# Which engine waits for the last output stores: five waits on ScalarE in place of seventeen on SyncE

## The chip, the cores and the metric

The kernel runs on one core of one Trainium2 chip. A core has five engines with an instruction stream each: TensorE (PE, matrix products), VectorE (DVE), ScalarE (ACT), GpSimd (POOL) and SyncE (SP, which here only issues transfers and waits). They meet only through semaphores. Transfers run on DMA engines; SyncE and ScalarE each issue them into a queue of their own. The metric is the device time of one execution in microseconds, the median of several runs. Before the change it is 99.43 us.

## The reference

The inputs are x of 2048 x 640, wqkv of 640 x 1920 and wo of 640 x 640, all bf16. What is computed is a block of linear attention with 32 heads of 20 columns:

```python
qkv = (x @ wqkv).reshape(B, S, 3, H, Dh).transpose(2, 0, 3, 1, 4)
q, k, v = qkv[0], qkv[1], qkv[2]
phi = lambda t: where(t > 0, t + 1, exp(t)) + 1e-6
pq, pk = phi(q), phi(k)
kv  = einsum("bhsd,bhse->bhde", pk, v)
z   = einsum("bhsd->bhd", pk)
num = einsum("bhqd,bhde->bhqe", pq, kv)
den = einsum("bhqd,bhd->bhq", pq, z)[..., None] + 1e-6
out = (num / den).transpose(0, 2, 1, 3).reshape(B, S, D) @ wo
```

The output is 2048 x 640 in bf16, 2.62 MB.

## The kernel before

The 2048 rows are cut into 16 tiles of 128 rows (`st` = 0 to 15). The stages are: loading x, also transposed, and the weights; the keys and phi(k); the product of x with phi(k), summed over all rows; the queries and phi(q) with the denominators; a small matrix that joins kv and wo; and at the end the output tiles, phi(q) divided by the denominator times that small matrix.

Every instruction is recorded in a plan, class `Plan`, before any is emitted. `add` takes the engine, the tiles that are read and written, and whether it is a transfer. It works out which earlier instructions have to be over, and puts a wait only for those that the engine does not know to be over already. What an engine knows lies in `P.known[engine]`: for each semaphore the value that it has waited for, directly, or because an instruction that it waited for had itself waited for it. Each transfer has a semaphore of its own, which stands at 16 when all of it has landed. `emit` then writes out each engine's list in the order in which it was recorded: SyncE, GpSimd, ScalarE, VectorE, TensorE.

The output stage is what matters here. `out_tile` handles tiles 0 to 14: two products into two PSUM banks (`out_mm`, line 576), two copies into the staging buffer `osb[st % 4]` (`out_evac`, line 599 on ScalarE, line 602 on VectorE), and one store of 160 KB from SyncE's queue (`out_dma`, line 587). `out_last` handles tile 15 in four column ranges and two stores: columns 0 to 480 (120 KB) from SyncE's queue, and columns 480 to 640 (40 KB) from ScalarE's queue. Those are 17 stores, and `out_dma` notes the key of each in the list `out_keys`.

There are four staging buffers. So a copy for tile `st` has to wait until the store of tile `st - 4` has landed, and ScalarE, which copies a part of every tile, thereby comes to know that the stores of tiles 0 to 11 have landed. It does not come to know it of tiles 12, 13 and 14, nor of the two stores of tile 15.

After all lists are emitted, the last loop of the function (lines 730 to 732) adds a wait for each of the 17 stores to SyncE's program. The compiler puts two of these waits into one instruction where it can; in the profile line 732 has 9 instructions. ScalarE's program ends with the issue of the 40 KB store.

Of the kernel before, what the change touches and what calls it, by code (L numbers as in the profile page):

```python
# [84 lines left out]
def bass_standalone__linear_attn_block__prompt_kernel(nc, x, wqkv, wo, out):  # L85
# [15 lines left out]
    with contextlib.ExitStack() as ctx:  # L101
# [38 lines left out]
        P = Plan(nc, es)  # L140
# [588 lines left out]
            P.emit(name, eng)  # L729
        for key in out_keys:  # L730
            op = P.writers[key]
            nc.sync.wait_ge(P.sem_obj[op.sem], op.val)


# [26 lines left out]
```

## Time and profile before

| what | value |
|---|---|
| time, median of 3 runs | 99.43 us (99.40 to 99.69) |
| profiled execution, its own time | 99.56 us |
| profiled execution, span from first to last instruction of the kernel | 98.3 us |
| granted TensorE clock | 1.000 |
| TensorE busy | 95.1 us, 97% of the span |
| VectorE busy | 63.7 us, 65% |
| ScalarE busy | 48.8 us, 50% |

The profiled execution took 1.26 us more than its span: the span holds the kernel's own instructions, the time also holds something of what the runtime does ahead of them and behind them. The profile was taken by the hardware on one execution. The names PEq, ACTq, SPq and so on stand for an engine's sequencer, which carries out waits and issues transfers; such instructions are not counted as busy time. EVENT_SEMAPHORE is a wait as an instruction of its own, DMA_DIRECT2D is the issue of a transfer.

### The profile page before, as it was taken

What the parts mean: (1) busy time and instruction counts of PE and PEld (TensorE: products, weight loads), DVE (VectorE), ACT (ScalarE), POOL (GpSimd) and SP (SyncE); (2) the same over time, 40 slices, a digit from 0 to 9 for tenths busy, and PEclk for the clock granted to TensorE, in tenths of its full rate; (3) what the DMA queues carried; (4) which work ended last, traced back from release to release, by engine and by line L of the source; (5) the groups of instructions that cost most, each with busy time, mean ns of one, the idle gap of its engine ahead of it and who ended that gap; (6) DMA issues with size and microseconds to landing.
All of it is one profiled execution on the core that took longest, in us unless ns stands there. A gap on an engine that the chain in (4) does not pass through costs nothing.

```text
span 98.3 us, 1814 instructions
## 1 busy us (share of the span) xinstructions
PE 95.1 (97%) x694; PEld 61.2 (62%) x699; DVE 63.7 (65%) x124; ACT 48.8 (50%) x93; POOL 4.7 (5%) x19
## 2 busy tenths in 40 slices
PE   6999999999999999999999999999999999999991
PEld 2467777777755444445687867655557677777771
DVE  5314998888899439997839836758999206272222
ACT  5116455544526120005806456796988765453532
POOL 6500000000000000000000520000000000000000
DMA  2999999999998294000340023313200335532334
GB/s 48 320 269 194 238 157 111 350 366 360 316 169 108 21 239 80 0 0 0 63 77 7 0 63 93 94 32 86 79 0 0 133 74 168 205 117 87 130 133 137
DMA packets 26369, 12.60 MB, mean 128 GB/s; under 512 B 18553, under 2 KB 26361, under 8 KB 26361
## 3 DMA queue, kind: packets, MB, share of 16 engines
q1 hardware_dynamic: 25640, 11.87, 50.2%
q10 hardware_dynamic: 720, 0.61, 1.9%
q8 instruction: 5, 0.08, 0.3%
q14 instruction: 4, 0.02, 0.1%
HBM read 5.90 MB, written 2.62 MB: 87 GB/s over the span
## 4 chain that ended last, share of the span: by engine, by line
PE 95%; ACT 2%; issue 0%
PE ps L293 23%; PE ps L576 22%; PE ps L354 22%; PE ps L317 21%; PE ps L283 3%; ACT w2g L483 2%; PE ps L445 1%; PE ps L544 1%; PE ps L200 1%; PE ps L472 1%; ACT osb L599 0%
## 5 line engine op out<-in xcount | busy, mean ns | idle before, releaser
L317 PE MATMUL ps<-pk,xn 128*128 128x480 bf16 (+1 forms) x160 | 23.2, 299 | 0.0
L293 PE MATMUL ps<-wk,xT 128*128 128x320 bf16 x160 | 22.8, 303 | 0.0
L354 PE MATMUL ps<-xT,wqn 128*128 128x512 bf16 x95 | 22.0, 379 | 0.4 <-issue 0.2
L576 PE MATMUL ps<-w2p,pq 128*128 128x320 bf16 (+2 forms) x170 | 22.1, 291 | 0.0
L293 PEld LDWEIGHTS ps<-wk,xT 128*128 128x128 bf16 x160 | 15.6, 98 | 6.8 <-DMA wk<-in_wqkv_dram 0.9
L576 PEld LDWEIGHTS ps<-w2p,pq 128*128 128x128 bf16 x170 | 15.9, 98 | 6.2 <-issue 0.2
L317 PEld LDWEIGHTS ps<-pk,xn 128*128 128x128 bf16 x160 | 13.6, 98 | 9.4 <-issue 0.3
L362 ACT ACTIVATE eq<-ps 128x512 bf16<-128x512 f32 x20 | 11.9, 597 | 13.8 <-PE ps L354 13.6
L354 PEld LDWEIGHTS ps<-xT,wqn 128*128 128x128 bf16 x100 | 11.5, 118 | 9.1 <-issue 0.3
L306 ACT ACTIVATE ek<-ps 128x640 bf16<-128x640 f32 x16 | 11.2, 704 | 10.7 <-PE ps L293 10.1
L599 ACT CAST osb<-ps 128x320 bf16<-128x320 f32 (+2 forms) x27 | 11.0, 413 | 9.7 <-PE ps L576 9.0
L311 DVE SCALAR_TENSOR_TENSOR pk<-ps,ek 128x640 bf16<-128x640 f32 x16 | 13.2, 825 | 0.5
L569 DVE TENSOR_TENSOR pq<-pq,rd 128x512 bf16<-128x512 bf16 x20 | 7.3, 418 | 4.2 <-DMA rd<-rdc 4.2
L375 DVE TENSOR_SCALAR eq<-eq 128x512 bf16<-128x512 bf16 x20 | 5.8, 288 | 5.9 <-ACT eq L362 5.8
L602 DVE CAST osb<-ps 128x320 bf16<-128x320 f32 (+1 forms) x7 | 3.2, 456 | 8.7 <-PE ps L576 8.7
L308 DVE TENSOR_SCALAR ek<-ek 128x640 bf16<-128x640 bf16 x16 | 5.2, 325 | 5.3 <-ACT ek L306 5.1
L366 ACT ACTIVATE rq<-ps 128x512 bf16<-128x512 f32 x13 | 7.7, 592 | 0.0
L339 ACT CAST pt<-ps 128x480 bf16<-128x480 f32 x4 | 2.2, 562 | 8.2 <-PE ps L317 8.1
L379 DVE TENSOR_TENSOR pq<-eq,rq 128x512 bf16<-128x512 bf16 x13 | 5.5, 426 | 1.1 <-ACT rq L366 0.7
L388 DVE TENSOR_TENSOR za<-pk 128x1280 f32<-128x1280 bf16 x4 | 5.8, 1482 | 0.0
L382 DVE SCALAR_TENSOR_TENSOR pq<-ps,eq 128x512 bf16<-128x512 f32 x7 | 4.8, 692 | 0.2
L388 DVE TENSOR_TENSOR za<-za 128x1280 f32<-128x1280 f32 x3 | 4.4, 1486 | 0.0
(37 smaller groups left out, 36.7 us busy)
## 6 DMA issues: line engine op xcount, KB each, us to landing
out_dram<-osb SPq DMA_DIRECT2D x15, 160.0 KB, 1.8
xn<-in_x_dram SPq DMA_DIRECT2D x2, 640.0 KB, 8.9
xn<-in_x_dram SPq DMA_DIRECT2D x1, 960.0 KB, 7.0
wqn<-in_wqkv_dram SPq DMA_DIRECT2D x1, 800.0 KB, 5.6
wv<-in_wqkv_dram SPq DMA_DIRECT2D x5, 150.0 KB, 5.1
wog<-in_wo_dram SPq DMA_DIRECT2D x2, 375.0 KB, 5.3
w2p<-w2g SPq DMA_DIRECT2D x10, 75.0 KB
rd<-rdc SPq DMA_DIRECT2D x8, 64.0 KB, 2.1
```

The source lines that it names most:

```text
L293: r = e.matmul(bank(b + h, HALF), xT[:, c * S + 128 * st:c * S + 128 * st + 128], wk[:, c * D + HALF * h:c * D + HALF * (h + 1)], start=(c ...
L306: P.add("act", lambda e: e.activation(fold(t[:, :]), two_banks(b), ACTF.Exp), reads=banks + ["table"], writes=[("ek", st % 3)])
L311: P.add("dve", lambda e: e.scalar_tensor_tensor(fold(pk[:, st * D:(st + 1) * D]), two_banks(b), 0.0, fold(t[:, :]), ALU.max, ALU.add), rea ...
L317: return e.matmul(bank(d // PB[h], PW[h], off=PW[h] * (d % PB[h])), xn[:, st * D + 128 * d:st * D + 128 * d + 128], pk[:, st * D + PO[h]:s ...
L354: r = e.matmul(bank(b), wqn[:, d * D:(d + 1) * D].rearrange("p (q c) -> p c q", c=NC_)[:, c, :], xT[:, d * S + BK * sbk:d * S + BK * (sbk ...
L362: P.add("act", lambda e: e.activation(t[:, :], bank(b), ACTF.Exp), reads=[("bank", b), "table"], writes=[("eq", i)])
L366: P.add("act", lambda e: e.activation(r[:, :], bank(b), ACTF.Relu), reads=[("bank", b), "table"], writes=[("rq", i)])
L375: P.add("dve", lambda e: e.tensor_scalar(t[:, :], t[:, :], 1.0, 1e-6, ALU.min, ALU.add), reads=[("eq", i)], writes=[("eq", i)])
L388: P.add("dve", lambda e: e.tensor_tensor(d_ap, a, b, ALU.add), reads=ra + rb, writes=[dst])
L569: P.add("dve", lambda e: e.tensor_tensor(v, v, rd[i][:, BK * h:BK * (h + 1)], ALU.mult), reads=[("rd", i, 2 * h), ("rd", i, 2 * h + 1), (" ...
L576: r = e.matmul(bank(b, hi - lo), pq[:, c * S + 128 * st:c * S + 128 * st + 128], w2p[:, c * D + lo:c * D + hi], start=(c == 0), stop=(c == ...
L599: P.add("act", lambda e: e.copy(osb[j][:, lo:hi], bank(b, hi - lo)), reads=[("bank", b)], writes=keys)
```

## The change

The loop at the end of the function no longer waits on SyncE. For each of the 17 stores it asks whether ScalarE's knowledge already covers the store's landing; if so, no wait is written, and if not, ScalarE waits. What is left is five waits at the end of ScalarE's program, behind the issue of the 40 KB store. SyncE's program ends with the issue of the 120 KB store.

```diff
         for key in out_keys:
             op = P.writers[key]
-            nc.sync.wait_ge(P.sem_obj[op.sem], op.val)
+            if P.known["act"].get(op.sem, 0) >= op.val:
+                continue
+            nc.scalar.wait_ge(P.sem_obj[op.sem], op.val)
```

## The prediction

> **What bounds the kernel now.** I read the page first, for the span and the chain that ended last.
>
> ```profile
> span 98.3 us, 1814 instructions
> ...
> PE   6999999999999999999999999999999999999991
> ...
> PE 95%; ACT 2%; issue 0%
> ```
>
> TensorE fills every slice but the first and the last, and the chain that ended last is 95% TensorE. The change touches no TensorE instruction and nothing that one waits for. So only the last slice, some 2 us in which TensorE is done, can move. Next I read the instructions in order of time from 96.3 us on.
>
> ```profile
> 96.12 0.20 PE L576 MATMUL ps<-w2p,pq 128*128 128x80 bf16 x1
> 96.18 0.24 DVE L602 CAST osb<-ps 128x80 bf16<-128x80 f32 x1
> 96.36 0.23 ACT L599 CAST osb<-ps 128x80 bf16<-128x80 f32 x1
> 96.36 0.33 SPq L587 DMA_DIRECT2D out_dram<-osb  x1
> 96.67 0.35 ACTq L587 DMA_DIRECT2D out_dram<-osb  x1
> ```
>
> The last issue is ScalarE's, over at 96.67 + 0.35 = 97.02. Behind it only waits stand: line 732's own instructions, SyncE's waits in that stretch, and the issues with their times to landing.
>
> ```profile
> L732 SPq EVENT_SEMAPHORE  x9: 17/28/28, 96.8 to 98.3; - x9
> ```
>
> ```profile
> SPq L732 <- DMA out_dram<-osb: 0.5, 1, 0.5
> ```
>
> ```profile
> out_dram<-osb SPq DMA_DIRECT2D x1, 120.0 KB, 1.7
> out_dram<-osb ACTq DMA_DIRECT2D x1, 40.0 KB, 1.6
> ```
>
> The columns of the first are shortest/median/longest in ns and first and last start. The nine waits begin at 96.8 and the last at 98.3, where the span ends. The 40 KB store, issued at 96.67, lands 1.6 us later: 98.26 in the trace's landings (the 120 KB store at 98.09). Two steps of 16 and 28 ns follow, SyncE's last wait starting at 98.276 and over at 98.304. The landing of ScalarE's store, not the number of waits, ends the program.
>
> **Behind the span.** The profiled execution took 99.56 us, so 1.26 us lie around the span. Besides the views, the trace keeps a time for each semaphore update. Semaphore 2, which no line of the kernel uses, goes up nine times ahead of the kernel, nine times around its end and nine times after it (ns from the span's start, as the trace records them):
>
> ```
> ahead    -370  -336  -298  -254  -231  -118   -80   -46     1
> end     96498 97295 97333 97377 98436 98479 98517 98551 98599
> after   99387 99421 99460 99504 99527 99626 99664 99698 99745
> ```
>
> I read each line as a barrier in which the five engines sign in one after another and four of them again on the way back. In the line "end" the second step comes 271 ns after ScalarE's last issue (97024), and the fifth 132 ns after SyncE's last wait (98304), about 1.1 us behind the fourth. So the second signer is ScalarE and the fifth, the turning point, is SyncE; the first (96498, just behind the last matmul's update at 96336) is TensorE. Which of VectorE and GpSimd is third doesn't matter. From 98569 to 99163 a block of semaphore updates follows that the kernel does not make, the resets of about 50 semaphores by each engine; the last 50 end at 99163, long behind the others (98970), and belong to the first signer by their numbers (semaphores up to 53). So what follows starts from step nine.
>
> **The change part by part.**
>
> SyncE loses 9 wait instructions. Seven were over by 97.62, below 98.26; their 17 to 28 ns each are covered by the flight of the last stores. The eighth (98.104) is covered by the landing at 98.26. Removed: 0 on the path, except the last, which is replaced. Nothing is queued behind SyncE's waits in the kernel, so its earlier end releases no transfer. Its own sign-in stays behind the fourth.
>
> ScalarE gains five waits, 3 instructions if two are again put into one. Behind them on ScalarE stands no kernel instruction: its last copy and its last issue are ahead. So no copy, issue or buffer comes later. The waits for tiles 12 to 14 are for landings up to 97.27 (the third of them), covered by 98.26. The wait for the last store then ends as SyncE's did: 16 + at most 28 ns behind the landing, 98.304. Shown for single waits of the plan, the two engines' prices agree (17 ns on both):
>
> ```profile
> L81 ACTq EVENT_SEMAPHORE  x35: 17/17/17, 2.7 to 96.6; - x35
> L81 SPq EVENT_SEMAPHORE  x10: 17/17/17, 56.0 to 96.3; - x10
> ```
>
> So the span stays at 98.3, plus or minus 0.03.
>
> What moves is the last arrival at the barrier. Now SyncE comes last and is the fifth: after 132 ns to its step, four steps back, 98599 - 98436 = 163 ns. Together 295 ns. Afterwards ScalarE comes last and is the second: x ns to its step, then seven steps. The trace has no barrier that only ScalarE held up; the nearest rows are the two unhindered passes, where second to ninth took 1 + 336 = 337 and 99745 - 99421 = 324 ns, mean 330. (The step after the turn takes 113 and 99 ns there, since that engine has just signed; 43 where it had long been waiting, as at "end".) The difference is 330 + x - 295 = 35 + x ns.
>
> The x is not shown behind a wait. From below: one instruction, the shown gap of 40 ns behind an issue of ScalarE's and 17 ns, gives 57, so +0.09 us. From above: the 271 ns that ScalarE took in this trace, behind its issue, gives +0.31. SyncE's 132 behind a wait is the like case on the other engine and gives +0.17; ScalarE is quicker through the runtime's instructions elsewhere (from its step to its first reset 99 ns, SyncE 133), which would make x 99 and the sum +0.13. I take x = 115, between these two, because they are the rows behind a wait or a step; the 271 I put down to a store just issued, whose first packet started only at 97.55. That gives +0.15 us: 99.56 + 0.15 = 99.71 for the profiled execution, which stood 0.13 above the median of the runs; on the median 99.43 + 0.15 = **99.58**.
>
> Everything behind the ninth step keeps its length, since TensorE's resets are the longest and start from there; the covers that SyncE and ScalarE have for their own resets are 0.2 us and more.
>
> The Trainium skill speaks against this change as well: "Runtime: NRT & Kernel Launch", section "The ~15µs preamble/postamble breakdown", has the barrier as a serpentine over the five engines at 44 ns a hop, eight hops, about 355 ns. The trace's passes agree in the whole (371 and 358 ns) but not step by step (23 to 113 ns). By equal hops the move from fifth to second costs three hops, 132 ns, and the time would be 99.56; the page doesn't say which engine is where.
>
> **The rivals.**
>
> A: ScalarE's 271 ns are the runtime's work on ScalarE, whatever stands ahead of it. For it: it is the only row of ScalarE's arrival. Against it: ScalarE's other turnarounds are shorter than SyncE's. The mechanism is in the second step of the barrier, its price 271 + 35 = 306 ns, time 99.74, slower by 0.31%. It decides from x = 263 on, where the sum reaches 0.298 us.
>
> B: the time ends with the kernel's last instruction, or the barrier is not on its path. For it: I can't place the two ends of the 1.26 us. Against it: 99.56 is longer than from the span's start to the ninth step at "end" (98.60), and nothing in the trace lies in the 1.2 us just ahead of the first instruction but that barrier and four transfers of 40 bytes. Then only the wait's 28 ns are in play: 99.43, within 0.03.
>
> C: SyncE's waits slow the last landing. For it: one 8 KB fetch of instructions starts at 98.173, between SyncE's last two waits, and the last two increments of the 40 KB store's semaphore come 26 and 40 ns after the one ahead, where the others stand 8 to 20 ns apart. If SyncE's shorter program moves that fetch behind the landing, some 26 + 40 - 2 x 10 = 46 ns come back: 99.53. With the lower bound of x (57, +0.09) as well it is 99.47. Against a real gain: that is still no time below 99.43, and no row shows a larger saving.
>
> D: the waits push ScalarE's closing instructions over an edge of its instruction memory, and a fetch comes between. The 8 KB fetches took 0.31 to 0.51 us during the kernel (47.9, 49.6 and 98.2 us). That gives 99.9 to 100.1. Against it: three instructions are few, and a page is fetched ahead.
>
> **How the numbers follow.** About 0.3%, 0.30 us, is what a measurement of this kernel can tell from no change. The main case has 0.57 of the chance, A 0.22, B 0.13, C 0.04, D 0.04. The main case reaches from 99.52 (x = 57) to 99.66 (x midway to A), with the scatter of a median of 3 (the runs shown lie 99.40 to 99.69) from 99.46 to 99.74, so about 0.05 of its chance falls beyond 99.73. A lies on that edge: some 0.15 of its 0.22 fall beyond, the rest on this side. With D and a little scatter, slower has 0.27. Faster has no mechanism among these; scatter below B, and what I have not seen, get 0.06. Same: 0.67. The range runs from 99.40, which holds B with little scatter, to 99.79, which holds A; D and the tails are left out, about 1.5 in 10.
>
> **What the profile after would show.** No SyncE instruction behind its issue at 96.4 and three ScalarE waits, the last starting at 98.28: the edit. The span at 98.3: the landing sets it. Semaphore 2: the fifth step right behind the fourth, the second one 115 ns behind ScalarE's last wait, and second to ninth in 324 to 340 ns. If the second comes 271 ns behind, A holds. If all this holds and the time doesn't move, B does. A fetch between ScalarE's last wait and the second step is D. The prediction is wrong if the last store lands at another time, or if the ninth step moves by 0.3 us or more.

## The result, and the profile after

The changed kernel takes 100.12 us, the kernel before 99.69 us (medians of 22 runs each; the 99.43 of the first three runs was on the low side). The ratio is 1.0047, with a 95% interval of 1.0026 to 1.0067: some 0.3 to 0.7 us slower. When it was run again beside the experiments the ratio was 1.0030 [1.0006, 1.0054]. The forecast was +0.15 us, counted as no difference, with 0.27 for slower. Single slow runs, over 1.5% longer than the fastest of the same kernel, are left out of the ratios and of the means below.

Within the span nothing of weight moved. From the page of the changed kernel, the span, the engines' busy time and TensorE's slices:

```profile
span 98.3 us, 1813 instructions
...
PE 95.1 (97%) x699; PEld 60.8 (62%) x699; DVE 63.7 (65%) x124; ACT 48.8 (50%) x93; POOL 4.7 (5%) x19
...
PE   6899999999999999999999999999999999999991
```

Its last instructions in order of time, and the waits of its line 734 (shortest/median/longest in ns, first and last start):

```profile
96.31 0.33 SPq L587 DMA_DIRECT2D out_dram<-osb  x1
96.61 0.35 ACTq L587 DMA_DIRECT2D out_dram<-osb  x1
```

```profile
L734 ACTq EVENT_SEMAPHORE  x3: 17/38/38, 97.2 to 98.2; - x3
```

SyncE has nothing behind its issue at 96.31. ScalarE's three waits take the place of SyncE's nine, the last from 98.223 to 98.261, 21 ns behind the last landing at 98.202. The span is 98.26 us against 98.30. So all of the loss lies outside the span: the profiled execution took 99.86 us, 1.60 more than its span, where the one before took 1.26 more. Over the runs, time minus span is 1.65 us on average for the changed kernel and 1.27 for the kernel before (34 runs taken beside the first experiments). Both differences scatter much less than the times themselves, because most of the scatter is in the span: a run with a longer span has a longer time as well. That is why most readings below use this difference. A span is known to 0.1 us, so a single value is worth little; means over eight runs and more are used.

The trace's updates of semaphore 2, in ns from the span's start; "end" is the barrier behind the kernel, "close" the closing barrier behind the resets:

```
                  1     2     3     4     5     6     7     8     9
before  end   96498 97295 97333 97377 98436 98479 98517 98551 98599
after   end   96444 98370 98408 98452 98475 98573 98611 98645 98693
before  close 99387 99421 99460 99504 99527 99626 99664 99698 99745
after   close 99513 99547 99585 99629 99653 99751 99789 99823 99870
```

At the end of the changed kernel the second step is the late one, 109 ns behind ScalarE's last wait, and the seven steps behind it take 323 ns. From the last landing to the ninth step it is 98693 - 98202 = 491 ns against 98599 - 98260 = 339: +152 ns. That is the forecast. The rest comes later. The ninth step to the last step of the closing barrier takes 1177 instead of 1146 ns. And the time, 99.86, ends 0.01 us ahead of that last step, where in the kernel before 99.56 lay 0.185 us ahead of it. (Here and below the time is counted from the span's start. Where it really begins, no view shows; so only differences between kernels mean something in such a figure.) In sum 0.152 + 0.031 + 0.175 = 0.36 us; the means of time minus span give 0.38.

One row stands out in that last stretch. In the changed kernel's DMA queues between 99.5 and 100.3 us (packets, MB, share of the engines' time) there is one packet of 8 KB for instructions, from 99.82 to 100.16 us, still running at the last step of the closing barrier (99.87):

```profile
DMA packets 1, 0.01 MB, mean 10 GB/s; under 512 B 0, under 2 KB 0, under 8 KB 0
...
q14 instruction: 1, 0.01, 2.7%
```

In the kernel before a packet of the same size in the same queue runs from 98.17 to 98.48 us, and none comes later. The view between 96.5 and 98.3 us has it:

```profile
q14 instruction: 1, 0.01, 1.1%
```

So the suspicion: SyncE's program, nine instructions shorter, comes later to a place in its code at which something is fetched.

### The profile page after: what moved, and what is told of

It reads as the page before. It is cut to its first block, busy times and chain, and to the rows that moved or that the text cites. A ratio compares the mean times of both kernels' runs of the same rounds, so it can differ in the third digit from the quotient of the medians.

```text
span 98.3 us, 1813 instructions
## 1 busy us (share of the span) xinstructions
PE 95.1 (97%) x699; PEld 60.8 (62%) x699; DVE 63.7 (65%) x124; ACT 48.8 (50%) x93; POOL 4.7 (5%) x19
## 4 chain that ended last, share of the span: by engine, by line
PE 93%; DMA 3%; SPq 0%; DVE 0%; issue 0%; ACT 0%
PE ps L293 22%; PE ps L576 22%; PE ps L317 22%; PE ps L354 22%; DMA wk<-in_wqkv_dram 3%; PE ps L445 1%; PE ps L544 1%; PE ps L472 1%; SPq L241 0%; DVE xT L212 0%; ACT osb L599 0%; PE ps L200 0%
## 5 line engine op out<-in xcount | busy, mean ns | idle before, releaser
L354 PE MATMUL ps<-xT,wqn 128*128 128x512 bf16 x100 | 23.1, 379 | 0.0
L293 PE MATMUL ps<-wk,xT 128*128 128x320 bf16 x160 | 22.3, 299 | 0.4 <-DMA wk<-in_wqkv_dram 0.3
```

What stands on the lines that cost most here:

```text
L293: r = e.matmul(bank(b + h, HALF), xT[:, c * S + 128 * st:c * S + 128 * st + 128], wk[:, c * D + HALF * h:c * D + HALF * (h + 1)], start=(c ...
L354: r = e.matmul(bank(b), wqn[:, d * D:(d + 1) * D].rearrange("p (q c) -> p c q", c=NC_)[:, c, :], xT[:, d * S + BK * sbk:d * S + BK * (sbk ...
```

## The experiments

All change only the loop at the end of the function. "Early stores" are those of tiles 0 to 11, whose landing is long past when SyncE gets to the end; a wait for one of them is an instruction without a delay of its own. The compiler puts two waits into an instruction, so 2n waits are n instructions. The edits of "Both engines wait" and of the three kernels with added SyncE instructions are shown against the changed kernel, all others against the kernel before.

### The change again

No edit.

> The changed kernel again, beside the others of this set. Theory 1 (barrier): what lies behind the span grows because ScalarE signs second and not fifth; the ninth update of semaphore 2 comes 0.49 us behind the last landing, against 0.34 in the kernel before, +0.15 us, and that is the whole effect. Theory 2 (fetch): SyncE's program, nine instructions shorter, reaches the edge of its instruction page only in the runtime's closing instructions (in the changed trace an 8 KB fetch at 99.82 us, before at 98.17), and that adds 0.2 to 0.3 us on top, so +0.43 us in all and time minus span 1.55 to 1.85 us instead of 1.26.

Measured: ratio 1.0030 [1.0006, 1.0054], time minus span 1.66 us (1.43 to 1.78). Ninth step 492 ns behind the last landing; the 8 KB fetch at 99.89; the time ends 0.006 us ahead of the last step. Both extra parts come again. The barrier alone is not the whole effect.

### Both engines wait

```diff
+        for key in out_keys:
+            op = P.writers[key]
+            nc.sync.wait_ge(P.sem_obj[op.sem], op.val)
         for key in out_keys:
             op = P.writers[key]
             if P.known["act"].get(op.sem, 0) >= op.val:
                 continue
             nc.scalar.wait_ge(P.sem_obj[op.sem], op.val)
```

> SyncE keeps all seventeen waits (nine instructions) and ScalarE waits for the five as well. ScalarE arrives at the end as in the changed kernel, SyncE's program is as long as before. Barrier theory: the ninth update of semaphore 2 comes 0.49 us behind the last landing; time +0.15 us. Fetch theory: the 8 KB fetch is back at 98.2 us, under the flight of the last store, so its 0.2 to 0.3 us are gone and only the barrier's +0.15 us is left. If ScalarE's waits cost the whole 0.43 us by themselves, this kernel is +0.43 us too.

Measured: ratio 0.9998 [0.9973, 1.0022], time minus span 1.41 us (1.38 to 1.47). Ninth step 491 ns behind the last landing, exactly as in the changed kernel; the fetch at 98.11; the time ends 0.185 us ahead of the last step, as in the kernel before. With SyncE's nine instructions back, ScalarE's waits cost 0.14 us, about what the barrier's 152 ns ask for. The other 0.25 us go away, although these instructions hold up nothing: ScalarE's last wait ends at 98.348 us, SyncE's at 98.333.

### Five waits, on SyncE

```diff
         for key in out_keys:
             op = P.writers[key]
+            if P.known["act"].get(op.sem, 0) >= op.val:
+                continue
             nc.sync.wait_ge(P.sem_obj[op.sem], op.val)
```

> Only the five waits, but on SyncE (three instructions, six fewer than before); ScalarE's program as before. Barrier theory alone: nothing changes, 0.00 us, ninth update 0.34 us behind the last landing. Fetch theory: the fetch starts some six SyncE instructions later, behind the last wait and among the runtime's closing instructions (between 98.7 and 99.6 us), and the time rises by up to 0.3 us though the barrier is as before.

Measured: ratio 1.0036 [1.0007, 1.0066], time minus span 1.68 us (1.63 to 1.72). Leaving out waits that had long been satisfied, on the same engine, costs 0.4 us. But not in the way that was expected. The three waits of this kernel:

```profile
L734 SPq EVENT_SEMAPHORE  x3: 17/28/28, 97.8 to 98.8; - x3
```

SyncE signs at the barrier 545 ns behind the end of the last one (98.790 to 99.335), where it took 132 before. The fetch comes at 99.93 and is over by 100.27, ahead of the closing barrier's last step (100.65). So besides the late fetch there is a stand of 413 ns in SyncE's instruction stream, and here it is exposed: it is the whole of the 0.4 us.

It is in the trace of the kernel before as well. The waits of line 732 fall into these stretches (96.7 to 97.0 and 97.0 to 97.7 us):

```profile
L732 SPq EVENT_SEMAPHORE  x4: 17/28/28, 96.8 to 97.0; - x4
```

```profile
L732 SPq EVENT_SEMAPHORE  x3: 28/28/28, 97.4 to 97.6; - x3
```

Between the fourth, over at 96.984, and the fifth at 97.438 SyncE stands for 0.454 us. The fifth waits for the stores of tiles 12 and 4, and the later of the two had landed at 94.56 by the trace's landings. Neighbouring waits follow each other after 0.042 us. So some 0.41 us of this gap belong to no semaphore. It cost nothing there because the last store landed only at 98.26.

### Five waits on TensorE

```diff
-            nc.sync.wait_ge(P.sem_obj[op.sem], op.val)
+            if P.known["act"].get(op.sem, 0) >= op.val:
+                continue
+            nc.tensor.wait_ge(P.sem_obj[op.sem], op.val)
```

> The five waits on TensorE, the first signer; SyncE's program as short as in the changed kernel. Barrier theory: all nine steps come behind TensorE's arrival, 0.37 us for the pass and about 0.16 us for its arrival behind a wait of about 0.05 us, so the ninth update 0.58 to 0.62 us behind the last landing, +0.24 to +0.28 us against before by the barrier. Fetch theory adds its 0.2 to 0.3 us as in the changed kernel: +0.45 to +0.55 us in all.

Measured: ratio 1.0031 [0.9996, 1.0065], time minus span 1.71 us, but from 1.48 to 1.94. Now all nine steps come behind TensorE's last wait: the first 216 ns behind it, the ninth 654 ns behind the last landing, 0.03 us more than expected. In the profiled execution the time ended 0.185 us ahead of the last step, as in the kernel before, so there only the barrier's part is seen. The scatter says that other runs paid more. The trace shows no fetch at the end of this one, so why the others did is open.

### Where the stand is: five, seven and fifteen wait instructions on SyncE

With n = 2, 4 and 12 instructions ahead of the five waits:

```diff
-        for key in out_keys:
-            op = P.writers[key]
+        for i in range(2 * n):
+            op = P.writers[out_keys[i % 12]]
+            nc.sync.wait_ge(P.sem_obj[op.sem], op.val)
+        for key in out_keys:
+            op = P.writers[key]
+            if P.known["act"].get(op.sem, 0) >= op.val:
+                continue
             nc.sync.wait_ge(P.sem_obj[op.sem], op.val)
```

> The five waits on SyncE with two instructions of long satisfied waits beside them: five wait instructions in all, where the kernel before has nine and the kernel with five waits on SyncE has three. With three, SyncE needed 545 ns from its last wait to its sign-in at the barrier instead of 132, and time minus span was 1.68 instead of 1.27 us. Theory F (a fetch of the page that holds the runtime's closing instructions; it is under way early only if SyncE has run far enough before the last landing): a step, so still about 545 ns and 1.68 us as long as the edge lies behind the last wait. Theory N (the programs are filled up to equal length with empty instructions that run behind the last wait, some 69 ns each): linear, 407 ns and 1.54 us.

> The same with four such instructions, seven wait instructions in all. Theory F: 545 ns and 1.68 us, or 132 ns and 1.27 us, nothing between. Theory N: 270 ns and 1.41 us.

> The five waits on SyncE with twelve instructions of long satisfied waits, fifteen in all, six more than the kernel before. Theory F: the fetch starts before 98.1 us, well ahead of the last landing; 132 ns from SyncE's last wait to its step and 1.27 us, as the kernel before. Theory N: 132 ns as well if the length before was already the full one, or a new stretch of empty instructions with up to 0.4 us.

Counted in the trace from the span's first, the issue of SyncE's last store is its 75th instruction in all these kernels, so the waits begin with the 76th. Starts in us, and the gap from the end of the 79th to the start of the 80th:

| kernel | SyncE instructions | 79th | 80th | gap | last landing | fetch | time minus span | ratio |
|---|---|---|---|---|---|---|---|---|
| before (nine) | 84 | 96.956 | 97.438 | 454 ns | 98.260 | 98.17 | 1.27 | |
| five | 80 | 97.990 | 98.470 | 452 ns | 98.148 | 99.09 | 1.30 | 1.0006 [0.9970, 1.0042] |
| seven | 82 | 97.540 | 98.023 | 455 ns | 98.835 | 98.90 | 1.28 | 1.0007 [0.9975, 1.0040] |
| fifteen | 90 | 97.453 | 97.944 | 463 ns | 98.783 | 98.59 | 1.27 | 1.0000 [0.9972, 1.0029] |

The gap is always between the 79th and the 80th instruction, whatever the 80th waits for. So it is tied to a place in SyncE's program. From its last wait to its step at the barrier SyncE took 171, 136 and 132 ns with five, seven and fifteen instructions. So theory N (407 and 270 ns with five and seven) falls. Theory F has a step, as measured, but with five it put the step behind the last wait (545 ns), where the stand lies ahead of that wait. With three waits the sign-in at the barrier would be the 80th, if it is the second instruction behind the kernel's last; that place is worked out from the 413 ns, since the trace does not list the runtime's instructions. With five the 80th is the last wait. The last store landed at 98.148 and the wait for it started only at 98.470, so that the span ends 0.350 us behind the landing, where it was 0.044 in the kernel before:

```profile
L737 SPq EVENT_SEMAPHORE  x5: 17/28/28, 96.6 to 98.5; - x5
```

Time minus span can't show these 0.31 us, which lie within the span, and the interval of the ratio is too wide for them; the ninth step, 684 ns behind the last landing (339 before), does. With seven and more the stand is over before the last store lands.

### The changed kernel with one, two and three more SyncE instructions

With n = 1, 2 and 3:

```diff
+        for i in range(2 * n):
+            op = P.writers[out_keys[i % 12]]
+            nc.sync.wait_ge(P.sem_obj[op.sem], op.val)
         for key in out_keys:
             op = P.writers[key]
             if P.known["act"].get(op.sem, 0) >= op.val:
                 continue
             nc.scalar.wait_ge(P.sem_obj[op.sem], op.val)
```

> The changed kernel with one long satisfied wait instruction at the end of SyncE's program (76 SyncE instructions in the profile instead of 75). Shown so far: ahead of its 80th instruction SyncE stands for 0.41 us whatever it waits for, and an 8 KB fetch follows 0.6 to 0.9 us later. Behind the kernel the sign-in at the barrier is the second instruction, so here the 79th... the count being 76 it is the 78th, and the 80th is the second behind it. Theory E (the edge, with the fetch that follows it, hurts where it comes so late that the fetch is still running at the end): the fetch starts about 0.1 to 0.3 us earlier than in the changed kernel's 99.8 to 99.9 us; time minus span between 1.40 and 1.66 us. If only one more instruction already takes the edge ahead of the closing barrier: 1.40 us. If the length of SyncE's program has nothing to do with it: 1.66 us with the scatter of the changed kernel.

> The same with two such instructions (77). The sign-in is then the 79th SyncE instruction and the 80th comes right behind it. Theory E: the 0.41 us stand between SyncE's step, the fifth, and its resets of semaphores 207 to 255, which began 0.145 us behind the fifth step in the changed kernel and here begin about 0.55 us behind it; that is covered, since TensorE's resets end 0.8 us behind the fifth step; the fetch starts by 99.6 us and is over ahead of the end; time minus span 1.40 us with little scatter. If SyncE's length has nothing to do with it: 1.66 us.

> The changed kernel with three long satisfied wait instructions added at the end of SyncE's program, which ends at 96.9 us all the same. The barrier is held by ScalarE as in the changed kernel: ninth update 0.49 us behind the last landing, +0.14 us of time minus span. The changed kernel's time minus span scattered from 1.35 to 1.87 us (median about 1.66), and a fetch of 8 KB stood at 99.8 us, behind SyncE's last step of the closing barrier. Theory F: with three instructions more the fetch starts before SyncE's step of the closing barrier and is covered there: 1.41 us, with little scatter, about 0.25 us less than the changed kernel. If the fetch has nothing to do with it: 1.66 us with the same scatter.

| SyncE instructions added | landing to ninth step | fifth step to SyncE's resets | fetch | last step of all | time ends ahead of it by | time minus span | ratio |
|---|---|---|---|---|---|---|---|
| 0 (the change) | 491 ns | 145 ns | 99.82 | 99.870 | 0.010 us | 1.65 | 1.0047 [1.0026, 1.0067] |
| 1 | 491 ns | 563 ns | 100.24 | 100.174 | -0.076 us | 1.54 | 1.0024 [0.9996, 1.0052] |
| 2 | 491 ns | 671 ns | 99.79 | 100.044 | 0.014 us | 1.52 | 1.0018 [0.9993, 1.0044] |
| 3 | 491 ns | 163 ns | 98.30 | 100.034 | 0.184 us | 1.38 | 0.9992 [0.9965, 1.0019] |

Three instructions that hold up nothing, at the end of a program that is over at 97.1 us, take 0.27 us off the time minus span. It is their number that counts and not when SyncE gets done: with two it gets done 0.07 us earlier, and half of the loss is still there (1.52 us). The fetch of the kernel with three, between 98 and 99 us:

```profile
q14 instruction: 1, 0.01, 2.8%
```

By the count of above, the 80th instruction is SyncE's sign-in with three added, and the stand passes while it waits for ScalarE anyway. With one and two it lies between the sign-in and SyncE's resets: these begin 0.56 and 0.67 us behind the fifth step instead of 0.145. That was expected of the second, though with 0.55; the other 0.12 us are open. They still end ahead of TensorE's resets (99.45 against 99.46 us with two). With none added, no step and no reset of SyncE's is late, so in the changed kernel the stand itself is nowhere on the path. It was not expected that so little is won with two: 1.52 us, not 1.40.

What hurts there shows when the time is set beside the end of the fetch:

| profiled execution | fetch over at | behind the last step by | time | fetch's end less time |
|---|---|---|---|---|
| the change | 100.162 | 0.292 us | 99.86 | 0.302 us |
| the change again | 100.233 | 0.297 us | 99.93 | 0.303 us |
| one added | 100.549 | 0.375 us | 100.25 | 0.299 us |
| two added | 100.322 | 0.278 us | 100.03 | 0.292 us |

In all four the time keeps the same distance from the end of the fetch, within 0.011 us, while its distance from the last step varies by 0.09. In the ten other profiles the time is 0.184 to 0.191 us less than the last step. So the time follows the later of the two, the closing barrier or the fetch. The kernel with five waits on SyncE fits: its fetch comes as late, but so does its closing barrier, and the time goes by the barrier (0.190 us). What costs time in these four is therefore the late fetch, not the stand; that rests on four profiles, and no run moved the fetch alone.

### Five waits on VectorE and on GpSimd

SyncE's program is kept at its length with nine instructions for early stores. The edit for VectorE; for GpSimd the last line has `nc.gpsimd`.

```diff
-        for key in out_keys:
-            op = P.writers[key]
-            nc.sync.wait_ge(P.sem_obj[op.sem], op.val)
+        for i in range(18):
+            op = P.writers[out_keys[i % 12]]
+            nc.sync.wait_ge(P.sem_obj[op.sem], op.val)
+        for key in out_keys:
+            op = P.writers[key]
+            if P.known["act"].get(op.sem, 0) >= op.val:
+                continue
+            nc.vector.wait_ge(P.sem_obj[op.sem], op.val)
```

> The five waits on VectorE, with SyncE's program as long as in the kernel before (nine long satisfied wait instructions), so that the edge plays no part. Barrier theory: VectorE signs fourth; from the fourth step to the ninth the passes before and after took 255 and 241 ns; with some 0.04 us for the wait and 0.10 to 0.15 us to its step the ninth update comes 0.42 to 0.45 us behind the last landing (before 0.34, with ScalarE 0.49), and time minus span is 1.33 to 1.37 us (before 1.27, with ScalarE 1.41). If VectorE is third, 0.46 to 0.49 us and 1.37 to 1.40 us. If the order of the engines doesn't matter and only the waiting engine's own way to the barrier does, no such order between the engines shows.

> The five waits on GpSimd, SyncE's program padded to the length of the kernel before. Barrier theory: GpSimd signs third; from the third step to the ninth the passes took 299 and 285 ns; the ninth update 0.46 to 0.50 us behind the last landing, time minus span 1.37 to 1.41 us. If GpSimd is fourth, 0.05 us less.

On VectorE the fourth step is the late one, 141 ns behind its last wait; the ninth step comes 458 ns behind the last landing, time minus span is 1.34 us, the ratio 1.0018 [0.9991, 1.0046]. On GpSimd the third step is late, and it comes 533 ns behind the last wait, far more than on any other engine: ninth step 885 ns behind the landing, time minus span 1.77 us, ratio 1.0061 [1.0036, 1.0086]. The order of the engines is as forecast; VectorE's 458 ns lie 8 ns above the forecast range; GpSimd's own way to the barrier was badly underestimated (0.46 to 0.50 us were expected). VectorE's kernel also shows the place in SyncE's program once more, since its nine waits are all for early stores, in the stretches 96.5 to 97.2 and 97.2 to 98.2 us:

```profile
L732 SPq EVENT_SEMAPHORE  x4: 27/28/28, 97.0 to 97.2; - x4
```

```profile
L732 SPq EVENT_SEMAPHORE  x5: 28/28/28, 97.7 to 97.9; - x5
```

Four, a gap of half a microsecond, five: the 80th again, and no store is waited for.

## Why the prediction was wrong

**What held.** The span stays at 98.3 us, set by the landing of ScalarE's store. ScalarE is the second signer, VectorE the fourth and SyncE the fifth, shown by the kernels that let each of them come last. The x behind a wait is 109 ns (115 were taken), the seven steps behind it take 323 ns (330 were taken), the whole term is 152 ns (150 were forecast). That it fits so well is partly luck: these two make it 13 ns smaller, and ScalarE's last wait made it 15 ns larger, since it ended 59 ns behind the landing and not 44, which had been put at no difference (a wait for two stores took 38 ns on ScalarE, 28 on SyncE). With SyncE's program at its old length or three instructions longer than the change leaves it, time minus span is 1.41 and 1.38 us against 1.27: 0.11 to 0.14 us, so this term is also about what the time pays.

**What failed.** The sentence on what SyncE loses: "Removed: 0 on the path, except the last, which is replaced." The nine instructions took no time on the path, but they brought SyncE past its 79th instruction before the end. Without them the place with the stand of 0.41 us moves into the runtime's closing instructions, and the fetch of 8 KB, which started at 98.17 us, starts at 99.82. So the statement "Everything behind the ninth step keeps its length" falls: the time's end moved by 0.175 us against the last step. Its reason, that TensorE's resets are the longest, held, and so did the covers for the other engines' resets; what it left out is that the time can follow something else than the barriers, here the fetch. In the means this missing term is 1.65 - 1.41 = 0.24 us, with 1.38 for the other kernel 0.27. It is larger than the one that was worked out. The stretch between the barriers grew by 0.031 us as well, but it did so too with SyncE's nine instructions kept.

**What could have been seen.** The 0.454 us between SyncE's fourth and fifth wait stood in the trace of before, at waits for stores that had landed 2.4 us and more earlier. The prediction noted only that seven waits were over by 97.62 and that their own 17 to 28 ns are covered; the gap it did not mention. It asked of each instruction how long it took and not why it started when it did. Of the fetch at 98.17 it asked whether it delayed the store (rival C), and of the instruction memory only whether ScalarE's program, which grows, crosses an edge (rival D). The program that shrinks was the one.

**The rivals.** A falls: 271 ns is ScalarE's way to the barrier behind an issue, 109 behind a wait. B falls: the time moves with what comes behind the span. C was right that SyncE's shorter program moves the fetch, and took it for a gain. That falls: the last store still landed 1.587 us after the start of its issue, against 1.591 before. The increments that C read as delayed by the fetch are the third last and the last (26 and 40 ns, with 9 between), and without a fetch near it the last one still comes 33 ns behind the one ahead in the changed kernel. D had a fetch as the cause, on the wrong engine and at 0.04 of the chance; that its 99.9 to 100.1 us come near the measured time is luck.

**The size.** Barrier 0.14 to 0.15 us, SyncE's shorter program about 0.25 us: 0.38 us by the means of time minus span, within the interval of the ratio (0.26 to 0.67 us of 99.69). Of the 0.54 us between the forecast of 99.58 and the measured 100.12, another 0.26 are the base: the median of three runs was 99.43, that of 22 is 99.69.

**What the place may be.** The Trainium skill, "Runtime: NRT & Kernel Launch", section "Instruction fetch mechanics", says that an engine fetches its program in blocks of 16 KiB, that the next block is fetched while the current one runs, and that crossing a border is mostly hidden. In this case's traces the fetches of the queue concerned are of 8 KB, and SyncE's 0.41 us is hidden only where the barrier waits longer for something else. That the stand is such a crossing is argued and not shown: the place is fixed by the instruction count, and in the seven kernels with a wait there a fetch starts 0.6 to 0.9 us behind that wait's start. Nor does the trace say whose program the packet holds; that it moves with the length of SyncE's is what the runs show.

**What stays open.** Why the end of the time waits for the fetch, and whether it does so in runs that were not profiled. The scatter speaks for it: time minus span varies by 0.18 us and more between the runs of the change, of the kernels with one and two added instructions and of the one with the waits on TensorE, and by 0.12 at most in the others. But in the profile of the kernel with the waits on TensorE, which has the short SyncE program too, there is no late fetch on record, and its 0.185 us are those of the barrier. Why the stretch between the barriers takes 1174 to 1177 ns in the change and in the kernel with both engines' waits, and 1141 to 1153 in the others, is open too.

None of these kernels is faster than the one before.

## What to carry to other kernels

Taking out an instruction that costs no time can still cost time, because everything behind it in its engine's code moves: here nine satisfied or covered waits less cost 0.25 us. Where an engine ends its program early, ask what of its remaining code, the runtime's included, now runs at the very end, and look in the trace for gaps that no semaphore explains. And let the engine that signs last at the end barrier be the one that waits last: here that was SyncE, at 0.07 us less than VectorE, 0.14 less than ScalarE, and more for the others.

## What the runs showed of the hardware

- A place in an engine's code can cost 0.41 us by itself. SyncE stood before its 80th instruction for 0.452 to 0.463 us in all seven kernels that had a wait there, where 0.042 is usual.
- The time follows what is last, the closing barrier or an instruction fetch: in four profiles it was 0.292 to 0.303 us less than the end of a late fetch, in ten 0.184 to 0.191 less than the barrier's last step.
- From the end of its last wait to its step at the end barrier an engine took 109 ns (ScalarE), 132 (SyncE; 171 where the stand came just ahead of the last wait), 141 (VectorE), 216 (TensorE) and 533 (GpSimd). Behind the issue of a store ScalarE took 271.
- The closing part of the time is steady enough to measure tens of nanoseconds: time minus span of the kernel before had means of 1.270, 1.267 and 1.266 us in three sets of 28 to 34 runs, while its times ran from 99.3 to over 100 us.
